# Mixture-of-experts kernel: the expert pipeline runs one expert ahead instead of two, scale factors are spread on VectorE in three pieces, token transposes go by DMA, and the second expert's weights are split inside the routing

## The chip, the core and the metric

The kernel runs on one core of a Trainium2 chip. The metric is the device time of one execution in microseconds (us): 732.28 us is the median of three runs of the kernel before (731.65 to 732.44). Of the core's engines the text says PE for TensorE's matmuls (PEld its weight loads), DVE for VectorE, ACT for ScalarE, POOL for GpSimd and SP for SyncE, whose queue issues the plain DMAs.

## What is computed

Three stages follow each other (sizes: 4 batches, 8 heads, 768 steps, head size 48, so 3072 tokens of 384 numbers; 8 experts of 384 tokens each):

```
# 1 linear attention with decay w and bonus u, per batch and head
y[t] = r[t] @ (state + (u*k[t]) v[t]^T);  state = w*state + k[t] v[t]^T
# 2 greedy routing: all (token, expert) logits in falling order; a token goes to its
#   first expert that still holds fewer than 384 tokens; then per expert
h = max(x[mask] @ w1[e], 0);  x2[mask] = h @ w2[e]
# 3 a shared network with three input matrices (given as 64-bit floats)
out = max(x2 @ v1, x2 @ v2, x2 @ v3) @ w_out
```

## The kernel before

**Halves.** Every product of stages 2 and 3 is made of three fp16 products: a matrix is scaled by a power of two and split into a high half (ACT, `scale=s`) and a low half (DVE, raw times s minus the high half). `product` (L802) multiplies high by high, low by high and high by low. The scale of a matrix needs the largest of its sums of squares over all 128 partitions. `Scales.spread` (L388) finds it with PE: `turn` transposes a column of 128 numbers into a row (L395), DVE takes its maximum (L397), `share` multiplies the one number with a row of ones to bring it to all partitions (L401), and `powering` (L413) makes the power of two with five or six tiny DVE operations.

**Weights.** `weight(e, which)` (L571) prepares one of the two matrices of an expert, as a list of pieces: four looks (ACT squares, L569), the scale, then five or seven splits (high halves L612 on ACT, low halves L615 on DVE). `double(i)` (L626) does the same for one of the shared matrices, with integer operations on DVE that turn 64-bit floats into 32-bit ones (L657 to L672). A `Feed` (L459) holds such pieces in one order; the code around it runs pieces by a budget (`take`), and `ahead` issues the loads of their 768 KB blocks on SP into four slots.

**Order of the work.** In the attention (24 steps, one batch and chunk each) a feed spreads, over steps 1 to 22, both matrices of expert 0, two shared matrices and both matrices of expert 1. Then `Routing.run` (L1284) makes three rounds (`round`, L1078), a chain of small DVE, PE and ACT operations, then `settle` (L1157), which ends with the token lists `ids` (L1221) and a flag; `gather(0)` fetches expert 0's tokens by indirect DMA on POOL, and every engine goes through a branch on the flag (`tc.If`, L1297), whose body is skipped. `idle` puts steps of `inputs` (the scale of the tokens) between the operations of a round. `plan` (L738) builds the feed of what is left: the third shared matrix, w_out, and the weights of experts 2 to 7.

`Experts.run` (L907) then computes. `first(e)` is x @ w1 (72 matmuls of 128x128 by 384), `second(e)` is h @ w2 (72), `third(e)` the three shared matrices (162), `fourth(e)` w_out (54). `turn(e)` (L774) transposes an expert's gathered tokens: nine PE transposes of f32 blocks (L786), then halves on ACT and DVE out of PSUM (L798, L799). Expert 0 and 1 are done to `second` ahead of the loop; in iteration e of the loop (L965) `third(e)` is interleaved with `first(e+2)`, then come `second(e+2)` and `fourth(e)`. The scale of x2 (L861) uses `spread` as well. `side` runs pieces of the feed by a pace worked out from due times, `flush` all that is left up to a tag.

Of the kernel before, what the change touches and what calls it, by code (L numbers as in the profile page):

```python
# [377 lines left out]
class Scales:  # L378


    def __init__(self, tc, pool, K):
        self.nc, self.pool, self.K, self.n, self.psum = tc.nc, pool, K, 0, None
# [5 lines left out]
    def spread(self, peak, then):  # L388
# [15 lines left out]
        return [turn, share]  # L404

# [53 lines left out]
class Feed:  # L459


    SLOTS, AHEAD = 4, 6
# [5 lines left out]
    def add(self, tag, items, early=2):  # L468
# [8 lines left out]
        self.plan += items  # L477

# [37 lines left out]
    def take(self, tag, budget, slot=None, time=1.0, apart=1.0):  # L516

        self.spare = min(self.spare, 0.0) + budget
        self.now += time
        while self.left(tag) and self.spare > 0.3:  # L520
            pe = self.items[self.at][2]
            if pe and (self.now < self.ready or slot not in (None, pe)):
                return
            self.run()
            self.ready = self.now + apart
# [8 lines left out]
class Experts:  # L534
# [4 lines left out]
    def __init__(self, ctx, tc, K, w1, w2, vs, wo, x_dram, out):  # L539
# [4 lines left out]
        self.fix = ctx.enter_context(tc.tile_pool(name="fixed", bufs=1))  # L544
        self.sc = Scales(tc, ctx.enter_context(tc.tile_pool(name="scales", bufs=1)), K)
# [16 lines left out]
    def peak(self, x):  # L562
        p = self.sc.tile()
        self.nc.vector.tensor_reduce(p, x, AX.X, OP.max)
        return p

# [4 lines left out]
    def weight(self, e, which):  # L571

        nc = self.nc
        st = {}
# [16 lines left out]
        def peak():  # L591
            st["peak"] = self.peak(st["peaks"])

        def scale(top):
            st["s"], st["f"] = self.sc.power(top, 3, square=True)
# [12 lines left out]
        def split(n):  # L608
            def go():
                if n < len(parts):  # L610
                    raw, (hi, _) = part(*parts[n])
                    nc.scalar.activation(hi, raw, AF.Copy, scale=st["s"])  # L612
                if n:
                    raw, (hi, lo) = part(*parts[n - 1])
                    nc.vector.scalar_tensor_tensor(lo, raw, st["s"], hi, op0=OP.mult, op1=OP.subtract)  # L615
# [5 lines left out]
        turn, share = self.sc.spread(lambda: st["peak"], scale)  # L621
        return ([(look(j), False, [blocks[j // 2]], 0.9) for j in range(4)] + [(peak, False, blocks, 0.2)]
                + [(turn, 4, blocks, 0.2), (share, 2, blocks, 0.8)]
                + [(split(n), False, uses(n), 0.6 + 0.3 * which) for n in range(len(parts) + 1)])

    def double(self, i):  # L626
# [6 lines left out]
        st, bits = {}, {}  # L633
# [7 lines left out]
        def magnitude(j):  # L641
            a = bits[j] = self.wp.tile([128, 768], I32, name="da", bufs=2)
            nc.scalar.activation(a.bitcast(F32), pair(j)[1].bitcast(F32), AF.Abs, scale=65536.0)
# [5 lines left out]
        def shift(j):  # L649
            def go():  # L650
                total(j - 1)
                if j == 0:
                    magnitude(0)
# [3 lines left out]
                nc.vector.tensor_scalar(x, x, 2.0, None, op0=OP.max)  # L657
# [3 lines left out]
        def low(j):  # L661
            def go():
                if j + 1 < nb:
# [12 lines left out]
        def last():  # L676
            total(nb - 1)

        def peak():
            st["peak"] = self.peak(st["peaks"])  # L680

        def scale(top):
            st["s"], f = self.sc.power(top, 2, square=True, field=self.vf[:, i:i + 1] if i < 3 else None)
            if i == 3:
                self.wof = f
# [13 lines left out]
        turn, share = self.sc.spread(lambda: st["peak"], scale)  # L699
        near = [[blocks[j]] + blocks[j + 1:j + 2] for j in range(nb)]  # L700
        return ([(f(j), False, b, 1.1) for j in range(nb)
                 for f, b in ((shift, blocks[j:j + 1]), (low, near[j]), (sign, blocks[j:j + 1]))]
                + [(last, False, [], 0.1), (peak, False, [], 0.2), (turn, 4, [], 0.2), (share, 2, [], 0.8)]
                + [(split(j), False, [], 0.9) for j in range(nb + 1)])

# [679 lines left out]
```

## Time and profile before

| | |
|---|---|
| median of three runs | 732.28 us |
| the profiled execution: time, span | 732.94 us, 731.2 us |
| attention, up to the logits (L352) | 193 us of the span |
| routing, up to the token lists (L1221) | 193 to 225 us |
| first expert matmul to the last PE work | 231.8 to about 724 us |
| PE, DVE, ACT, POOL busy | 93%, 56%, 44%, 33% of the span |
| mean granted TensorE clock | 0.947 of 2.4 GHz |

The profile is one execution taken by the hardware profiler. Times count from the span's start. The chain that ended last is followed back from the last instruction, at each step to what released it or to the instruction before it on its engine.

### The profile page before, as it was taken

How to read it: one execution, taken by the hardware profiler on the slowest of the kernel's cores; microseconds unless marked ns; L12 is line 12 of the kernel's file. 1: busy time of each engine (PE TensorE's matmuls, PEld its weight loads, DVE VectorE, ACT ScalarE, POOL GpSimd, SP SyncE). 2: the span in 40 equal slices, each digit the busy share in tenths (PEclk: the TensorE clock that was granted, in tenths of full speed). 3: DMA queues.
4: the chain of work that ended last, by engine and by line, in shares of the span. 5: the costliest groups of instructions: out<-in, count | busy, mean ns of one | idle time of the engine just before them, and what ended most of it. 6: DMA issues, size and time to landing. Idle time of an engine off the chain costs nothing.

```text
span 731.2 us, 14572 instructions
## 1 busy us (share of the span) xinstructions
PE 680.0 (93%) x5891; PEld 456.6 (62%) x5891; DVE 411.7 (56%) x954; ACT 322.1 (44%) x657; POOL 238.6 (33%) x264
## 2 busy tenths in 40 slices
PE   5898888999748999999999999999999999999996
PEld 4687667788636755555665666666566665666663
DVE  6779989788673767865453453453535344332120
ACT  3454343454313576655553554544555343232221
POOL 5889777787004200210220220221121021121222
PEclk8999998799756999999999999999999999999999
DMA  5976745562404222421230230321202000000000
GB/s 157 308 230 194 241 138 181 187 199 72 151 1 134 90 85 86 162 87 44 77 119 12 109 118 1 112 83 44 91 30 87 0 33 1 1 34 1 33 1 32
DMA packets 37962, 68.86 MB, mean 94 GB/s; under 512 B 4608, under 2 KB 25216, under 8 KB 37888
## 3 DMA queue, kind: packets, MB, share of 16 engines
q1 hardware_dynamic: 34816, 58.42, 25.0%
q0 software_dynamic: 3072, 9.44, 3.8%
q8 instruction: 48, 0.79, 0.4%
q14 instruction: 26, 0.21, 0.1%
HBM read 58.41 MB, written 9.44 MB: 93 GB/s over the span
## 4 chain that ended last, share of the span: by engine, by line
PE 61%; DVE 3%; issue 2%; ACT 1%; DMA 1%; POOL 1%; POOLq 0%; ACTq 0%; DVEq 0%
PE pg L807 28%; PE ps L807 22%; PE px L893 8%; PE px L401 1%; DVE w L615 1%; PE px L786 1%; DMA stage<-in_moe_w_out_dram 1%; ACT w L612 0%; DVE xt L799 0%; DVE top L877 0%; PE px L395 0%; POOL out_dram L898 0%; DVE x2s L857 0%; POOL gt L880 0%; DVE ht L835 0%
## 5 line engine op out<-in xcount | busy, mean ns | idle before, releaser
L807 PE MATMUL pg<-x2s,v 128*128 128x384 f16 x1296 | 216.8, 326 | 0.0
L807 PEld LDWEIGHTS <-v 128*128 128x128 f16 x1296 | 126.5, 98 | 83.2
L807 PEld LDWEIGHTS <-w 128*128 128x128 f16 x1242 | 115.7, 98 | 70.9 <-issue 1.9
L880 POOL TENSOR_TENSOR gt<-top,gt 128x384 f16<-128x384 f32 x48 | 45.6, 951 | 342.4 <-ACT gt L879 301.5
L877 DVE SCALAR_TENSOR_TENSOR top<-pg,sc,top 128x384 f32<-128x384 f32 x96 | 59.3, 618 | 125.4 <-PE pg L807 122.9
L807 PE MATMUL ps<-ht,w 128*128 128x384 f16 x576 | 95.6, 326 | 0.0
L807 PE MATMUL ps<-xt,w 128*128 128x384 f16 (+1 forms) x540 | 88.5, 317 | 0.8 <-DVE ht L835 0.6
L879 ACT ACTIVATE gt<-top 128x384 f16<-128x384 f32 x48 | 25.1, 523 | 139.3 <-DVE top L877 139.3
L615 DVE SCALAR_TENSOR_TENSOR w<-stage,sc,w 128x512 f16<-128x512 f32 (+1 forms) x80 | 74.2, 950 | 7.4 <-ACT w L612 7.3
L893 PE MATMUL px<-wo,gt 128*128 128x384 f16 x432 | 72.6, 326 | 0.0
L612 ACT ACTIVATE w<-stage,sc 128x512 f16<-128x512 f32 (+1 forms) x80 | 60.8, 797 | 9.6 <-DVE sc L430 9.2
L893 PEld LDWEIGHTS <-gt 128*128 128x128 f16 x432 | 41.8, 98 | 27.0
L569 ACT ACTIVATE junk<-stage 128x768 bf16<-128x768 f32 x64 | 53.4, 835 | 2.8 <-DMA stage<-in_moe_w_dram 2.2
L835 DVE SCALAR_TENSOR_TENSOR ht<-ps,ht 128x384 f16<-128x384 f32 x56 | 30.6, 554 | 32.6 <-ACT ht L834 32.6
L263 ACT ACTIVATE junk<-x 128x384 bf16<-128x384 f32 x24 | 12.6, 523 | 69.5 <-DVE x L262 67.7
L847 DVE TENSOR_REDUCE part<-ps 128x1 f32<-128x384 f32 x24 | 13.4, 556 | 51.4 <-ACT x L846 51.4
L226 PE MATMUL pA<-rt,kt 64*128 64x128 f32 x384 | 34.3, 314 | 7.8 <-DVE am L229 7.5
L898 POOL DMA_INDIRECT out_dram<-o,ids x24 | 23.4, 974 | 44.6 <-ACT o L896 44.6
L226 PEld LDWEIGHTS pA<-rt,kt 64*128 64x128 f32 x384 | 28.4, 212 | 14.3 <-DVE am L229 9.8
L229 DVE TENSOR_TENSOR am<-pA,mask 128x512 f32<-128x512 f32 x48 | 30.7, 680 | 8.9 <-PE pA L226 8.9
L875 ACT ACTIVATE top<-pg,sc 128x384 f32<-128x384 f32 x48 | 27.8, 579 | 16.6 <-PE pg L807 16.2
L202 POOL TENSOR_TENSOR bv<-v,bon 128x384 f32<-128x384 f32 x24 | 23.1, 964 | 31.0 <-DVE bon L200 28.5
(229 smaller groups left out, 916.8 us busy)
## 6 DMA issues: line engine op xcount, KB each, us to landing
stage<-in_moe_w_dram SPq DMA_DIRECT2D x41, 768.0 KB, 4.9
kn<-in_k_dram SPq DMA_DIRECT2D x24, 192.0 KB, 4.6
rn<-in_r_dram SPq DMA_DIRECT2D x24, 192.0 KB, 4.1
v<-in_v_dram SPq DMA_DIRECT2D x24, 192.0 KB, 3.1
rt<-in_rt_dram SPq DMA_DIRECT2D x48, 96.0 KB, 3.2
x_rows<-x SPq DMA_DIRECT2D x24, 192.0 KB, 2.6
stage<-in_moe_w_out_dram SPq DMA_DIRECT2D x3, 768.0 KB, 4.1
xg<-x_rows,ids POOLq DMA_INDIRECT x24, 4.6
```

The lines of the kernel that those rows point to most:

```text
L226: nc.tensor.matmul(pa[s][:, j, :], kt[FULL[s], j * C:(j + 1) * C], rt[FULL[s], j * C:(j + 1) * C], start=True, stop=True, skip_group_check ...
L229: nc.vector.tensor_mul(am[:, s], pa[s], self.mask[:, None, :].to_broadcast([128, NP, C]))
L569: self.nc.scalar.activation(self.K.junk, x, AF.Square, accum_out=total)
L612: nc.scalar.activation(hi, raw, AF.Copy, scale=st["s"])
L615: nc.vector.scalar_tensor_tensor(lo, raw, st["s"], hi, op0=OP.mult, op1=OP.subtract)
L807: nc.tensor.matmul(p[:, rows], w[:, wi, k, cols], x[:, xi, k, rows], start=k == 0 and wi + xi == 0, stop=k == kb - 1 and xi == 1, skip_gro ...
L835: nc.vector.scalar_tensor_tensor(h[:, 1, f], p, 0.0, h[:, 0, f], op0=OP.max, op1=OP.subtract)
L875: nc.scalar.activation(t, p, AF.Copy, scale=self.ratio[i])
L877: nc.vector.scalar_tensor_tensor(t, p, self.ratio[i], top, op0=OP.mult, op1=OP.max)
L879: nc.scalar.activation(gt[:, 0, g], top, AF.Copy)
L880: nc.gpsimd.tensor_sub(gt[:, 1, g], top, gt[:, 0, g])
L893: nc.tensor.matmul(p, gt[:, gi, g, a * 128:(a + 1) * 128], self.WO[:, wi, g, :], start=g == 0 and gi + wi == 0, stop=g == self.KG - 1 and ...
```

## The change

1. `weight(1, 0)` and `weight(1, 1)` leave the attention's feed. Their pieces (41) become `second_matrices`, run by `aside(pieces)`: 4, 2+7 and 3+11 pieces inside rounds 1, 2 and 3, and 11 between `gather(0)` and the branch; the last three go to the feed. There the scale still goes by PE (`fine`), but in eight small pieces; seven of the ten low halves go to POOL in two operations each. The steps of `inputs` that are left run after `gather(0)` too.
2. In the planned feed (`early` is False) scales go by `around`: a column maximum, four 32x32 DVE transposes, a row maximum (`collect`), one DVE transpose of the broadcast number and two copies (`share`), the power of two (`end`). The x2 scale does the same, and its halves become three more pieces, spread by `step()`.
3. `turn(e)` for e of 1 and more makes the halves first, in token order, and then three `dma_start_transpose` on SP (128 x 768 fp16 each).
4. The loop runs one expert ahead: `third(0)` alone, `first(e+1)` beside `third(e)` for e from 1 to 6. w_out is due 1.5, ahead of expert 2.
5. In `double`, the maximum with 2.0 moves from DVE to POOL for matrices of the planned feed.

```diff
+    def around(self, peak, powers, kind):
+        ... (a, c, d), b = self.blocks[kind], self.wide
+        def collect():
+            peak(a[:, :1])
+            for q in range(4):
+                nc.vector.transpose(b[:32, 32 * q:32 * q + 32], a[32 * q:32 * q + 32])
+            nc.vector.tensor_reduce(c[:32, :1], b[:32], AX.X, OP.max)
+        def share():
+            nc.vector.transpose(d[:32], c[:32, :1].to_broadcast([32, 32]))
+            nc.vector.tensor_copy(d[32:64, :1], d[:32, :1])
+            nc.vector.tensor_copy(d[64:, :1], d[:64, :1])
+        def end():
+            for _ in powers(d[:, :1]):
+                pass
+    def fine(self, peak, powers):
+        ...
+        return [start, turn, share] + [lambda: next(st["g"])] * 4 + [last]
...
+            if calm:
+                nc.gpsimd.tensor_scalar(t, raw, st["s"], None, op0=OP.mult)
+                nc.gpsimd.tensor_sub(lo, t, hi)
...
+    def second_matrices(self):
+        (look, scale, _, upper, lower), (look2, scale2, split2, _, _) = (self.weight(1, n, True) for n in range(2))
+        return (look + scale[:5] + look2 + scale[5:] + scale2[:2] + [upper(0), upper(1), lower(0, True), upper(2), lower(1, True),
+                upper(3), lower(2, True), upper(4), upper(5)] + [lower(n) for n in range(3, 6)] + scale2[2:] + [split2(n, True) for n in range(5)])
...
+        if not blocks:
+            for a in range(3):
+                t = self.act.tile([128, 2, DM], F16, name="xr", bufs=3)
+                nc.scalar.activation(t[:, 0], self.XG[e % 2][a], AF.Copy, scale=K.xs)
+                nc.vector.scalar_tensor_tensor(t[:, 1], self.XG[e % 2][a], K.xs, t[:, 0], op0=OP.mult, op1=OP.subtract)
+                nc.sync.dma_start_transpose(xt.rearrange("p t j n -> p (t j) n")[:, :, a * 128:(a + 1) * 128],
+                                            t.rearrange("p t n -> p (t n)"))
...
         for e in range(E):
-            n = e + 2
+            n = e + 1
-            first = self.first(n) if n < E else iter(())
+            first = self.first(n) if e and n < E else iter(())
...
-        self.idle(1 if src is self.K.raw else 3)
+        self.idle(1 if n == 0 else 0)
+        self.aside((4, 7, 11)[n])
...
         then()
         for _ in other:
             pass
+        aside(11)
+        self.aside = lambda pieces: None
         with tc.If(bad != 0) as _:
...
-    for which in range(2):
-        feed.add(0, X.weight(1, which))
```

## Rows read from the trace of the kernel before

**Rows 1.** The chain that ended last, shares of the span by engine and by line (the page's part 4).

```profile
PE 61%; DVE 3%; issue 2%; ACT 1%; DMA 1%; POOL 1%; POOLq 0%; ACTq 0%; DVEq 0%
PE pg L807 28%; PE ps L807 22%; PE px L893 8%; PE px L401 1%; DVE w L615 1%; PE px L786 1%; DMA stage<-in_moe_w_out_dram 1%; ACT w L612 0%; DVE xt L799 0%; DVE top L877 0%; PE px L395 0%; POOL out_dram L898 0%; DVE x2s L857 0%; POOL gt L880 0%; DVE ht L835 0%
```

**Rows 2.** Busy time of each engine in the expert stages: stretch, its length, then PE, PEld, DVE, ACT, POOL busy with instruction counts, granted clock, DMA share, GB/s.

```profile
231.70:721.00 489.30, 485.40 (x3082) 297.50 (x3082) 230.82 (x521) 224.86 (x434) 89.70 (x112) 1.00 0.18 59
```

**Rows 3.** The chain in one expert's turn, in order of time: start, length, what.

```profile
484.89 0.98 PE px L786 x9
...
488.80 4.39 PE pg L807 x27
...
507.92 0.31 PE px L401 x2
...
524.42 0.11 PE px L395
```

**Rows 4.** PE's groups from 246 us to the end: busy us, mean ns of one, idle before.

```profile
L401 PE MATMUL px<-sc,onesf 1*128 1x1 f32 x44 | 8.3, 256 | 0.7 <-DVE xt L799 0.7
L786 PE MATMUL px<-identf,xg 128*128 128x128 f32 x63 | 8.3, 274 | 0.9 <-DVE sc L416 0.9
L395 PE MATMUL px<-identf,sc 128*1 128x128 f32 x22 | 6.0, 272 | 0.1
```

**Rows 5.** The stretch after the first experts' matrices begin to interleave, columns as in rows 2.

```profile
276.00:309.00 33.00, 30.79 (x193) 18.96 (x192) 25.87 (x58) 22.09 (x40) 4.97 (x5) 1.00 0.41 138
```

**Rows 6.** The same stretch, the chain in order of time: the longest piece.

```profile
284.43 5.21 DMA stage<-in_moe_w_out_dram
```

**Rows 7.** The attention's steps 1 to 23, columns as in rows 2.

```profile
27.00:190.80 163.80, 149.00 (x2522) 125.12 (x2521) 138.18 (x245) 78.40 (x167) 124.79 (x107) 0.93 0.56 179
```

**Rows 8.** The nine of these steps in which DVE is busy for 95% or more, the sum over them.

```profile
sum 79.50, PE 70.48 PEld 59.58 DVE 78.43 ACT 35.31 POOL 59.43; mean PE 7.83 PEld 6.62 DVE 8.71 ACT 3.92 POOL 6.60
```

**Rows 9.** DVE's groups of the feed in the attention, 60 to 185 us, shapes apart: busy us, mean ns.

```profile
L615 DVE SCALAR_TENSOR_TENSOR w<-stage,sc,w 128x512 f16<-128x512 f32 x6 | 7.2, 1217 | 0.0
L615 DVE SCALAR_TENSOR_TENSOR w<-stage,sc,w 128x768 f16<-128x768 f32 x4 | 5.6, 1418 | 0.0
L397 DVE TENSOR_REDUCE sc<-pX 1x1 f32<-1x128 f32 x5 | 1.4, 275 | 1.0 <-PE pX L395 1.0
L423 DVE TENSOR_SCALAR sc<-sc 128x1 int32<-128x1 int32 x5 | 0.8, 154 | 0.2
```

**Rows 10.** The same operation in the expert stages, 400 to 600 us, where POOL is mostly idle.

```profile
L615 DVE SCALAR_TENSOR_TENSOR w<-stage,sc,w 128x512 f16<-128x512 f32 x21 | 15.6, 764 | 0.8 <-ACT w L612 0.7
```

**Rows 11.** POOL's groups in the attention, 60 to 185 us.

```profile
L126 POOL TENSOR_TENSOR rt<-rt,tr 128x512 f32<-128x512 f32 x16 | 24.3, 1521 | 0.0
L192 POOL TENSOR_TENSOR rk<-rk,ub 128x384 f32<-128x384 f32 x16 | 20.1, 1257 | 1.3
L183 POOL TENSOR_TENSOR kp<-kn,tkn 128x384 f32<-128x384 f32 x15 | 18.4, 1228 | 2.1 <-PE pK L281 2.1
L191 POOL TENSOR_TENSOR rk<-rn,kn 128x384 f32<-128x384 f32 x16 | 18.2, 1139 | 0.0
L202 POOL TENSOR_TENSOR bv<-v,bon 128x384 f32<-128x384 f32 x18 | 17.6, 978 | 26.1 <-DVE bon L200 23.5 <-DVE sc L564 2.6
```

**Rows 12.** The routing in order of time, merged instructions: start, length, engine, line, operation, [idle before].

```profile
200.49 0.58 PE L732 MATMUL px<-sc,onesf 1*128 1x1 f32 x2
...
207.32 0.58 PE L1147 MATMUL pt<-vals,onesf 96*128 96x16 f32 x2 [2.32 <-DVE sc L425]
207.94 0.17 DVE L1151 TENSOR_SCALAR cut<-pt 128x8 f32<-128x8 f32 x1 [0.45 <-PE pt L1147]
...
217.82 0.46 ACT L1175 ACTIVATE ahead<-later,heldc 96x200 f16<-96x200 f16 x1 [4.62 <-DVE heldc L1173]
...
221.05 1.19 POOL L1203 TENSOR_TENSOR rhs<-col,token 128x576 f16<-128x576 f16 x1 [36.03 <-ACT gap L1209]
...
224.86 0.18 DVE L1221 TENSOR_SCALAR ids<-pn 128x24 int32<-128x24 f32 x1 [0.29 <-PE pn L1219]
```

**Rows 13.** The branch behind the routing, on PE's queue: durations in ns (min, median, max), first and last start.

```profile
L1297 PEldq COMPARE_BRANCH  x1: 3563/3563/3563, 226.0 to 226.0; - x1
```

**Rows 14.** The chain at the second and third block of expert 0's tokens, in order of time.

```profile
234.90 0.46 issue
...
235.74 1.05 issue
```

**Rows 15.** DMA issues (the page's part 6): KB each, median us from issue to landing.

```profile
v<-in_v_dram SPq DMA_DIRECT2D x24, 192.0 KB, 3.1
kn<-in_k_dram SPq DMA_DIRECT2D x24, 192.0 KB, 4.6
stage<-in_moe_w_dram SPq DMA_DIRECT2D x41, 768.0 KB, 4.9
```

**Rows 16.** One `second` of expert 0 on PE (timeline): its 72 matmuls.

```profile
247.51 11.86 PE L807 MATMUL ps<-ht,w 128*128 128x384 f16 x72
```

**Rows 17.** What follows `third` (page, part 5): the evacuations of its PSUM banks on ACT and DVE, and the low half on POOL.

```profile
L875 ACT ACTIVATE top<-pg,sc 128x384 f32<-128x384 f32 x48 | 27.8, 579 | 16.6 <-PE pg L807 16.2
L877 DVE SCALAR_TENSOR_TENSOR top<-pg,sc,top 128x384 f32<-128x384 f32 x96 | 59.3, 618 | 125.4 <-PE pg L807 122.9 <-ACT top L875 1.0 <-PE px L395 0.8
L880 POOL TENSOR_TENSOR gt<-top,gt 128x384 f16<-128x384 f32 x48 | 45.6, 951 | 342.4 <-ACT gt L879 301.5 <-issue 40.9
```

More of the change, by code (lines that the diff above doesn't have):

```diff
@@ L459 @@
 class Feed:
[L462 removed]
+    SLOTS, AHEAD, LAG = 4, 6, 1.4
     def __init__(self):
@@ L560, in block, with scaled, peak, then @@
         return b
[L562 to L565, printed above, removed]
     def square(self, x, total):
         self.nc.scalar.activation(self.K.junk, x, AF.Square, accum_out=total)
-    def weight(self, e, which):
+    def scaled(self, st, column, powers, blocks):
+        if self.early:
+            def peak():
+                st["m"] = self.sc.tile()
+                column(st["m"])
+            def then(top):
+                for _ in powers(top):
+                    pass
+            turn, share = self.sc.spread(lambda: st["m"], then)
+            return [(peak, False, blocks, 0.2), (turn, 4, blocks, 0.2), (share, 2, blocks, 0.8)]
+        collect, share, end = self.sc.around(column, powers, "weights")
+        def done():
+            end()
+            self.mark(st)
+        return [(collect, st, blocks, 1.2), (share, False, blocks, 0.6), (done, False, blocks, 0.8)]
+    def mark(self, st):
+        st["sent"] = self.feed.now
+    def weight(self, e, which, parted=False):
         nc = self.nc
-        st = {}
+        st = {"sent": 0.0}
         if which == 0:
@@ L588, in go, with column, powers @@
                 self.square(blocks[j // 2].get()[:, j % 2 * 768:j % 2 * 768 + 768], st["peaks"][:, j:j + 1])
-            return go
[L591 to L595, printed above, removed]
+                if j == 3 and not self.early:
+                    self.mark(st)
+            return go
+        def column(out):
+            nc.vector.tensor_reduce(out, st["peaks"], AX.X, OP.max)
+        def powers(top):
+            yield from self.sc.powering(top, 3, True, st)
             st["w"] = self.wpool[e % 2].tile([128, 2, kb, n], F16, name=f"w{which}", bufs=1)
@@ L619, in uses @@
             return [blocks[parts[i][0]] for i in (n - 1, n) if 0 <= i < len(parts)]
[L621 to L624, printed above, removed]
+        looks = [(look(j), False, [blocks[j // 2]], 0.9) for j in range(4)]
+        if parted:
+            return (looks, [(x, False, blocks, 0.2) for x in self.sc.fine(column, powers)],
+                    lambda n, calm: (split(n, calm), st if n == 0 and not self.early else False, uses(n), 0.9),
+                    lambda n: (lambda: upper(n), False, uses(n), 0.7), lambda n, calm=False: (lambda: lower(n, calm), False, uses(n + 1), 0.8))
+        return (looks + self.scaled(st, column, powers, blocks)
+                + [(split(n), st if n == 0 and not self.early else False, uses(n), 0.6 + 0.3 * which)
+                   for n in range(len(parts) + 1)])
     def double(self, i):
@@ L677, in last, with column, powers @@
             total(nb - 1)
[L679 to L683, printed above, removed]
+            if not early:
+                self.mark(st)
+        def column(out):
+            nc.vector.tensor_reduce(out, st["peaks"], AX.X, OP.max)
+        def powers(top):
+            if i < 3:
+                st["f"] = self.vf[:, i:i + 1]
+            yield from self.sc.powering(top, 2, True, st)
             if i == 3:
-                self.wof = f
+                self.wof = st["f"]
         def halves(j):
@@ L697, in split @@
             return go
-        turn, share = self.sc.spread(lambda: st["peak"], scale)
         near = [[blocks[j]] + blocks[j + 1:j + 2] for j in range(nb)]
[L701 to L704, printed above, removed]
+        return ([(lambda: magnitude(0), False, blocks[:1], 0.3)] * (not early)
+                + [(f(j), False, b, 1.1) for j in range(nb)
+                   for f, b in ((shift, blocks[j:j + 1] if early else near[j]), (low, near[j]), (sign, blocks[j:j + 1]))]
+                + [(last, False, [], 0.1)] + self.scaled(st, column, powers, [])
+                + [(split(j), st if j == 0 and not early else False, [], 0.9) for j in range(nb + 1)])
     def room(self, i):
@@ L1326, in body @@
         feed.add(0, X.double(i))
-    for which in range(2):
-        feed.add(0, X.weight(1, which))
     feed.close()
@@ L1337, in body @@
     with ExitStack() as rctx:
-        routing.run(rctx, X.inputs(), X.sc, lambda: X.gather(0))
+        routing.run(rctx, X.inputs(), X.aside, X.sc, lambda: X.gather(0))
     X.open(ctx)
```

204 lines of the change are left out of this document (131 added, 73 removed).

## The prediction

> **What bounds the kernel now.** I read the chain that ended last first. PE is 61% of it, nearly all of that in lines 807 and 893, the expert products [rows 1]. Then the busy time of each engine in the expert stages: PE is busy for 485.4 of 489.3 us at full clock, DVE for 230.8 and ACT for 224.9, so DVE and ACT are under half used [rows 2]. The reader should see that two thirds of the kernel are a queue of PE work with almost no holes: there only two things give time back, PE instructions that vanish and the few holes. Next the attention. Over its steps 1 to 23 DVE is busy for 138.2 of 163.8 us, POOL for 124.8 [rows 7]; in nine steps, 79.5 us together, DVE is busy for 78.4 [rows 8]. So about half of the attention (79.5 / 163.8 = 0.49) is bound by DVE, the rest by POOL, PE and waits. Last the routing: a chain of small operations in which ACT and POOL idle for long stretches (4.6 us ahead of line 1175, 36 us ahead of line 1203) [rows 12], closed by a branch.
>
> The sum is made against the profiled execution's own time, 732.94 us (span 731.2 and 1.7 around it). The median of the runs is 0.66 us lower; I take the difference from it.
>
> **Token transposes leave PE.** Experts 1 to 7 have nine PE transposes each, 63 in all [rows 4]; nine take 0.98 us of the chain [rows 3]. 7 x 0.98 = **-6.9 us**. The halves stay: one ACT and one DVE operation per token block as before. The three DMA transposes per expert wait on SP behind the halves. For experts 2 to 7 they are issued inside `third(e)` for a `first` one iteration later, some 58 us of PE work (489.3 / 8 is 61); that hides any landing time seen here. Only expert 1 is tight: its cover is `second(0)`, 11.9 us [rows 16]. No row shows a DMA transpose. The nearest are plain transfers of the same 192 KB, which land in 3.1 to 4.6 us [rows 15]. In a pipeline the three land some 7 us after `first(0)` ends, with about 2 us for the halves: hidden. One after another it is 3 x 4.6 + 2 = 15.8, 3.9 us too late. I take 0 and keep 0 to 3.9.
>
> **Scales leave PE.** From the start of the expert stages there are 22 column transposes and 44 passes of the one-number matmul [rows 4]; one scale takes 0.11 + 0.31 us of the chain [rows 3]. 22 x 0.42 = **-9.2 us**. What DVE gets for it is about seven more operations per scale at some 0.15 us (the tiny-operation row of rows 9), 22 x 7 x 0.15 = 23 us more on an engine that has 258 us free in that stage [rows 2]: 0. No DVE transpose is in the trace; between the 0.15 of a tiny operation and the 0.28 of a 128-number maximum [rows 9] it changes nothing.
>
> **One expert ahead.** It moves PE work without changing its amount. Its effect is on due times: ahead of `third(0)` the feed now owes one shared matrix, before it was one shared matrix and w1 of expert 2. In the stretch where this crowded, PE is busy for 30.8 of 33.0 us [rows 5], and the chain there runs through ACT and DVE and a 5.2 us wait for a block of w_out [rows 6]. At most 2.2 us are to be had; since w_out now comes in `third(0)` and can block ACT in the same way, I take **-1.0** (0 to -2.2). The evacuation of `third`, 0.58 us on ACT and two of 0.62 on DVE [rows 17], fits the 4.39 us that PE needs for one group [rows 3], also where nothing is interleaved.
>
> **The attention without expert 1's weights.** DVE loses six low halves of 1.22 us, four of 1.42, and two scales of about 1.2 us (0.15 + 0.28 + five tiny ones) [rows 9]: 7.3 + 5.7 + 2.4 = 15.4 us. ACT loses eight looks and ten high halves, but is busy for 78 of 164 us [rows 7], so that counts for nothing. POOL's own work stays: a step has 1.52 + 1.26 + 1.23 + 1.14 + 0.98 = 6.1 us on POOL [rows 11], against 7.1 us for a mean step, so a step cannot shrink far. If DVE bound everything the gain would be 15.4; if POOL and PE took over at once it would be 0. The feed spreads what is left over the same steps, so I count the share of the time that DVE bounds: 15.4 x 0.49 = **-7.5** (0 to -15.4).
>
> **The routing with expert 1's weights.** Three costs, none of them in the trace as such.
> (a) In round 2, `share` and two power steps now stand ahead of `cut`. DVE must wait there for the one-number matmul, which PE runs behind the `pt` matmul; in round 1 of before such a pair follows by 0.5 us [rows 12]. With the two operations of 0.15 us `cut` comes at about 208.85 instead of 207.94: +0.9.
> (b) ACT's high halves and POOL's low halves fill idle time. Six high halves fit the 4.6 us ahead of line 1175 by a hair [rows 12]; POOL's three low halves should be done as line 1203 needs it. DVE's operations beside a busy POOL are longer: 1.22 against 0.76 us for the same 128x512 low half [rows 9, 10]. A dozen operations of settle by up to 0.25 us is 3 us; nothing slower is 0. I take +0.8, since most of settle's operations are far smaller than a low half.
> (c) Eleven pieces and the five last steps of the tokens' scale stand between `ids` and the branch, and that is no wait: each engine takes the branch only after them. DVE: five tiny ones 0.8, three low halves 2.3 [rows 10], the maximum 0.3; then PE's one-number matmul 0.6. PE's branch, at 226.0 before, starts at about 229.9, and it lasts 3.56 us [rows 13]. So the first transposes come 3.9 us later. About 2 us of that are given back, since PE afterwards waited 0.46 and 1.05 us for later token blocks, with a transpose between [rows 14], which will then lie there. ACT has two high halves of the second matrix to issue ahead of its own branch and may be later still. I take +2.3 (0 to 4).
> Sum **+4.0** (+1 to +7).
>
> **Sum.** -6.9 - 9.2 - 1.0 - 7.5 + 4.0 = -20.6. 732.94 gives 712.3 for a profiled execution, 732.28 gives **711.7 us**. All ends together: 732.3 - 6.9 - 9.2 - 2.2 - 15.4 + 1 = 699.6, and 732.3 - 6.9 - 9.2 + 7 + 3.9 = 727.1.
>
> **Rivals.**
> A. *The attention does not shrink* (0.13). For it: POOL's 6.1 us of a 7.1 us step, and the light steps that run with DVE far from full. Against: half of the time with DVE at 98%. Time 732.3 - 20.6 + 7.5 = 719.2.
> B. *DVE's whole time comes back and the routing hides the rest* (0.10). For it: the heavy steps dropped the granted clock (0.93 over the stretch [rows 7]), which evener steps would mend. Time 732.3 - 6.9 - 9.2 - 1.0 - 15.4 + 1 = 701.
> C. *The transposes of expert 1 land behind `second(0)`* (0.10). For it: no row bounds a transpose from above. Against: the plain transfers of rows 15. Time 715.6 by the rows' worst, about 725 at three times their time.
> The Trainium skill, VectorE: DVE Perf Modes, section The three transpose paths, gives 1309 ns for one 128x128 transpose by DMA against 390 on TensorE; an estimate from that page for 18 blocks in a row is 23.6 us, and expert 1 would be 13.7 us late, 725 in all; no row here shows it.
> D. *SP becomes the bound* (0.05), the one that ends slower. SP issues in order; if a transpose holds it, the blocks of the feed queue behind, ACT stands at a look or a magnitude whose block is not there, and PSUM isn't emptied. The one such wait in the trace is 5.2 us [rows 6]. PE has about three groups of PSUM, some 4.4 us, in hand, so it decides when a turn holds SP for some 8 us or more longer than a block's 4.9 us takes to land [rows 15]; with 5.2 us lost in each of six turns it is 31 us, 711.7 + 31 = 743.
> That part of the change doesn't do what it says is in (c): the last pieces lie behind the routing's waits, not in them. E. *POOL's low halves hold up settle* (0.05). For it: the longer low halves beside a busy POOL [rows 9, 10]. Against: POOL's three should end as settle begins. If six of settle's operations each wait for one POOL operation of 0.95 us [rows 17], (b) is 5.7 instead of 0.8, and the time 716.6.
> The Trainium skill, SBUF — State Buffer, section Who interferes with whom, speaks for E: a DVE operation with two SBUF inputs and a POOL operation that reads SBUF exclude each other for a whole instruction; the longer low halves agree with that, while by rows 9 and 10 alone the price is the 0.25 us each that (b) counts at most.
> That part of the change doesn't do what it says is in (c): the last pieces lie behind the routing's waits, not in them. The remaining 0.57 is the forecast, some 704 to 718.
>
> **How the numbers follow.** A measurement of this kernel tells about 0.2% (1.5 us) from no change. The range 702 to 722 takes in the forecast, A, E and the near part of C; it leaves out half of B, the far end of C and D, about 0.15. Faster needs over 1.5 us: all but D and a sliver, 0.93; within 0.2% 0.02; slower 0.05.
>
> **What would show it.** No L786 transposes for experts 1 to 7 and no one-number matmuls in the expert stages; that stretch, 489.3 us, near 472 plus any holes. The attention's end, at 193.0, near 185.5. `ids` some 1.7 us later after that end than the 31.8 us of before, and the first expert product 8 to 11 us after `ids` (6.7 before). PE without a hole at the start of `first(1)`. Wrong would be: an attention that ends at 192 (A) or 178 (B), a hole there (C), ACT waiting for stage blocks in each expert (D).

## The result

The changed kernel takes 740.81 us (median of 4 runs, 740.4 to 742.66), the kernel before 732.36 beside it (4 runs, 731.65 to 734.35): ratio 1.0116, 95% interval 1.009 to 1.0142 (as for all ratios here). It is slower by 8.5 us; 711.7 was forecast. The profiled execution took 740.82 us, its span 739.1.

**Four cuts through the span.** The line that copies the attention's last result, the one that makes `ids`, and the first expert product are in both traces. After the change, in order of time (start, length, engine, line, operation, what the engine had waited for):

```profile
181.28 0.33 ACT L352 ACTIVATE raw<-lg 128x192 f32<-128x192 f32 x1 [0.93 <-PE lg L306]
...
196.68 0.16 DVE L470 TENSOR_SCALAR sc<-py 128x1 int32<-128x1 int32 x1 [1.08 <-PE py L451]
...
196.94 0.16 DVE L1292 TENSOR_SCALAR cut<-pt 128x8 f32<-128x8 f32 x1
...
202.95 1.16 POOL L707 TENSOR_TENSOR w<-da,w 128x512 f16<-128x512 f32 x1 [2.16 <-ACT w L700]
...
203.10 1.03 DVE L1281 SCALAR_TENSOR_TENSOR pick<-pick,least 96x1 f32<-96x1 f32 x1
204.09 1.56 POOL L706 TENSOR_SCALAR da<-stage,sc 128x512 f32<-128x512 f32 x1
204.16 0.65 DVE L1284 TENSOR_TENSOR vals<-same,pick 96x16 f32<-96x16 f32 x1
...
205.96 1.14 DVE L1295 TENSOR_TENSOR pen<-nl,cut 128x192 f32<-128x192 f32 x1
...
207.14 0.73 DVE L1296 SCALAR_TENSOR_TENSOR nl<-pen,nl 128x192 f32<-128x192 f32 x1
...
216.59 0.18 DVE L1362 TENSOR_SCALAR ids<-pn 128x24 int32<-128x24 f32 x1 [0.30 <-PE pn L1360]
...
227.82 1.51 PE L925 MATMUL px<-identf,xg 128*128 128x128 f32 x6 [6.59 <-ACTq L1440]
...
229.49 1.13 PE L943 MATMUL ps<-xt,w 128*128 128x128 f16 x9 [0.16 <-ACT xt L934]
```

| part of the span | before, us | after, us | difference | forecast |
|---|---|---|---|---|
| start to the attention's end (L352) | 193.0 | 181.3 | -11.7 | -7.5 |
| to `ids` [rows 12] | 31.9 | 35.3 | +3.4 | +1.7 |
| to the first expert product | 6.9 | 12.9 | +6.0 | +2.3 |
| to the end of the span | 499.4 | 509.6 | +10.2 | -17.1 |

The forecast of the third row has some 2 us in it that PE was to get back just behind the first product. All ahead of the experts together gained 2.3 us, as against 3.5 forecast; the miss lies in the last row, 27.3 us.

**Where in the expert stage.** PE's products of the output matrix come once per expert. After the change three in a row start 58.50 us apart:

```profile
395.50 8.94 PE L1034 MATMUL px<-wo,gt 128*128 128x384 f16 x54
454.00 8.94 PE L1034 MATMUL px<-wo,gt 128*128 128x384 f16 x54
512.50 8.94 PE L1034 MATMUL px<-wo,gt 128*128 128x384 f16 x54
```

Before, they start 61.05 apart:

```profile
402.26 3.09 PE L893 MATMUL px<-wo,gt 128*128 128x384 f16 x18
...
463.31 3.09 PE L893 MATMUL px<-wo,gt 128*128 128x384 f16 x18
```

The 2.55 us per expert are a little more than the two PE terms promised (16.1 / 7 = 2.3). The loss is earlier. Windows of the changed kernel, columns as in [rows 2]:

```profile
229.50:255.50 26.00, 26.00 (x239) 19.38 (x239) 8.72 (x16) 7.48 (x16) 10.48 (x8) 0.93 0.39 100
255.50:288.00 32.50, 16.92 (x80) 8.60 (x79) 20.41 (x41) 15.32 (x28) 18.02 (x9) 0.73 0.31 106
288.00:300.20 12.20, 12.20 (x67) 6.91 (x67) 7.15 (x22) 2.65 (x7) 0.48 (x1) 0.88 0.11 41
300.20:324.00 23.80, 19.60 (x117) 11.12 (x116) 18.26 (x55) 14.11 (x25) 5.95 (x6) 1.00 0.36 63
324.00:345.90 21.90, 18.39 (x100) 10.16 (x100) 13.91 (x43) 12.37 (x24) 4.94 (x8) 0.92 0.41 136
232.00:345.00 113.00, 89.71 (x572) 53.14 (x570) 67.33 (x173) 51.48 (x97) 37.98 (x29) 0.89 0.33 91
345.90:660.00 314.10, 314.08 (x1933) 188.76 (x1931) 167.30 (x442) 156.07 (x305) 61.18 (x76) 1.00 0.26 74
```

and one of the kernel before:

```profile
232.00:345.00 113.00, 109.17 (x759) 69.47 (x757) 76.40 (x166) 67.30 (x130) 16.50 (x17) 0.99 0.29 91
```

From 346 us on PE has no hole at all. Between 232 and 345 it idles 23.3 us against 3.8, and runs at a granted clock of 0.89 against 0.99, so that busy time times clock is 79.8 against 108.1: 28.3 us of full-speed work less, which covers the 27.3 us. The reader should also see the row above the hole: in 229.5 to 255.5 PE is full while DVE works 8.7 us and ACT 7.5. The feed stands still, and then the work comes all at once. The longest waits of PE between 232 and 345 are for DVE, whose evacuations of PE's banks (`ht`) stand behind pieces of the feed:

```profile
PE ps L943 <- DVE ht L971: 10.1, 2, 9.9
PE pg L943 <- DVE ht L971: 4.7, 1, 4.7
```

### The profile page after: what moved, and what is told of

Same layout as the page of the kernel before. It is cut to its first block, busy times and chain, and to the rows that moved or that the text cites. A ratio compares the mean times of both kernels' runs of the same rounds, so it can differ in the third digit from the quotient of the medians.

```text
span 739.1 us, 14533 instructions
## 1 busy us (share of the span) xinstructions
PE 664.2 (90%) x5762; PEld 441.1 (60%) x5762; DVE 434.4 (59%) x1097; ACT 321.8 (44%) x657; POOL 275.3 (37%) x284
## 4 chain that ended last, share of the span: by engine, by line
PE 57%; DVE 4%; issue 3%; ACT 2%; POOL 2%; POOLq 0%; DVEq 0%; ACTq 0%
PE pg L943 26%; PE ps L943 23%; PE px L1034 8%; DVE top L1018 1%; ACT junk L633 1%; POOL da L751 1%; ACT w L700 0%; DVE da L780 0%; DVE wo L815 0%; DVE v L815 0%; POOL gt L1021 0%; POOL w L707 0%; POOL da L706 0%; DVE ht L971 0%; POOL out_dram L1039 0%
## 5 line engine op out<-in xcount | busy, mean ns | idle before, releaser
L943 PEld LDWEIGHTS <-w 128*128 128x128 f16 x1242 | 119.1, 100 | 91.9 <-issue 22.2
L943 PE MATMUL ps<-ht,w 128*128 128x384 f16 x576 | 97.8, 332 | 10.8 <-DVE ht L971 9.9
L709 DVE SCALAR_TENSOR_TENSOR w<-stage,sc,w 128x512 f16<-128x512 f32 (+1 forms) x73 | 66.3, 933 | 6.1 <-ACT w L700 6.1
L982 ACT ACTIVATE x<-ps 128x384 f32<-128x384 f32 x24 | 11.8, 490 | 52.7 <-PE ps L943 52.7
L226 PE MATMUL pA<-rt,kt 64*128 64x128 f32 x384 | 32.1, 303 | 1.7 <-DVE am L229 1.5
L126 POOL TENSOR_TENSOR rt<-rt,tr 128x512 f32<-128x512 f32 x22 | 32.7, 1485 | 1.7 <-DMA rt<-in_rt_dram 1.7
```

Source lines behind the costliest of these rows:

```text
L126: (engine or self.nc.gpsimd).tensor_mul(self.RT[i], self.RT[i], self.tr)
L226: nc.tensor.matmul(pa[s][:, j, :], kt[FULL[s], j * C:(j + 1) * C], rt[FULL[s], j * C:(j + 1) * C], start=True, stop=True, skip_group_check ...
L943: nc.tensor.matmul(p[:, rows], w[:, wi, k, cols], x[:, xi, k, rows], start=k == 0 and wi + xi == 0, stop=k == kb - 1 and xi == 1, skip_gro ...
```

## The experiments

A code reading gave the first theory. The pieces that the routing runs aside are taken out of order by the feed's `run`, which charges their cost to `spare`; `take` starts each side from the negative `spare`. Adding up the kernel's own costs, the account stands at -21.2 when the expert stages begin, and the sides run nothing until it is paid back. The ratios below are each with the kernel before on the same chip; its median there was 732.5 to 734.7 us.

**e1: the debt.** At the end of `aside`:
```
+        self.feed.spare = 0.0
```


> The changed kernel with one line more: after the pieces that run inside the routing the feed's budget is set back to 0. Theory 1 (debt: the 38 pieces run in the routing are charged to the budget, which stands at -21.2 as the expert stages begin, so no piece runs for some 26 us and then two shared matrices are crammed into the next 60): ACT and DVE work from the first expert on, PE's idle time of 23 us between 255 and 346 us falls to under 6, time 710 to 718 against 740.8. Theory 2 (the operations moved to POOL, some 2.2 us each, stand in the path of ACT and DVE): the holes stay with little less, time over 730.

**e2: GpSimd's part.** In the planned feed, GpSimd's maximum (L751) and the low halves of expert 1's second matrix back on DVE; the debt stays:
```
-                nc.gpsimd.tensor_scalar(a, a, 2.0, None, op0=OP.max)
+                nc.vector.tensor_scalar(x, x, 2.0, None, op0=OP.max)
-    [split2(n, True) for n in range(5)]
+    [split2(n, False) for n in range(5)]
```


> The changed kernel with the planned feed's POOL operations back on DVE: the maximum with 2.0 of the shared matrices, and the low halves of the second matrix of expert 1; the debt stays. Theory 1: the feed still idles for 26 us and is crammed after, only the chains get shorter, 732 to 739. Theory 2: the holes go, under 722.

**e3: both edits.**


> Both edits, budget set back to 0 and POOL's operations of the planned feed back on DVE. Theory 1: as e1 within 4 us, 708 to 717. Theory 2: as e2, and e1 well above both.

**e4: e1, and no pieces ahead of the branch.**
```
-        self.aside((4, 7, 11)[n])
+        self.aside((4, 7, 9)[n])
-        aside(11)
```
(and the start of the second matrix's scale goes with its splits into the planned feed.)


> The edit of e1, and the 11 pieces ahead of the branch (with the start of the second matrix's scale) left to the feed of the expert stages; only the steps of the tokens' scale stay ahead of the branch. If those pieces delay the branch, the stretch from the token lists to the first expert product falls from 12.8 us to 8 or less, and the time is up to 5 us under e1 unless the crowded feed gives it back. If the branch is slow for another reason (instruction fetch beside the block loads), the stretch stays over 11 us.

| | us, median | ratio (interval) | first product | from there to the span's end | PE idle in 232 to 345 |
|---|---|---|---|---|---|
| before | 732.36 | | 231.8 | 499.4 | 3.8 |
| after | 740.81 | 1.0116 (1.009 to 1.0142) | 229.5 | 509.6 | 23.3 |
| e1 | 728.58 | 0.993 (0.9895 to 0.9964) | 231.6 | 499.9 | 14.7 |
| e2 | 736.04 | 1.0023 (0.999 to 1.0055) | 228.5 | 506.0 | 20.3 |
| e3 | 725.41 | 0.986 (0.981 to 0.9911) | 231.6 | 492.3 | 11.0 |
| e4 | 737.5 | 1.0043 (1.0006 to 1.0081) | 224.7 | 512.3 | 26.1 |

The stages here and below are read from one execution each, and that can lie off the median: e1's took 733.2 us, 4.6 more than its median, e6's 3.5 less, and those of p1b, p2 and p3 3.1 to 4.0 less. The debt costs 12.2 us in the median, 9.7 in the expert stage. GpSimd's operations cost 3.6 in that stage with the debt (509.6 to 506.0) and 7.6 without (499.9 to 492.3); in the medians it is 4.8 and 3.2. Together the two are 17.3 of the 27.3, 15.4 in the medians; how they share it is known to some 4 us only. The expectations of e1, 710 to 718, and of e3, 708 to 717, fell; e2's, 732 to 739, held: the debt is the largest single cause, not the whole. e4 settles the routing's third term. Before the branch stand no pieces, and from `ids` (217.66) to the first product (224.65) there are 7.0 us again, 6 less than after. But the eleven pieces, put into the planned feed, cost more than that: the kernel is 8.9 us slower than e1. One window of e4:

```profile
255.00:270.00 15.00, 4.66 (x18) 2.25 (x18) 7.34 (x10) 5.22 (x9) 11.43 (x6) 0.66 0.42 139
```

PE works 4.7 of 15 us, with GpSimd the busiest engine.

**e5: the order.** e3, and the third shared matrix wholly ahead of w_out's first pieces:
```
-        parts = [(1, self.double(i), 0) for i in late]
+        parts = [(1, self.double(i), None) for i in late]
```


> The changed kernel without the debt, with the VectorE forms of e3 (725.4), and with all pieces of the third shared matrix ahead of the pieces of expert 1's second matrix, so that not two matrices fall before the second expert's last products. Theory: what is left of the loss is the order and the crowding of these pieces on VectorE: 716 to 721, the holes of 255 to 330 us down from some 14 to some 6 us. Rival: the holes are the price of having one expert's weights less ahead, wherever the pieces stand: 724 to 727, the holes only move.

**e6: e5 with e4's edit.**


> e5 and, as in e4, no pieces between ids and the branch (the start of the second matrix's scale goes into the planned feed with its splits). By the routing term: about 6 us from ids to the first product come back, so 6 us below e5 if the planned feed has room for the 11 pieces (then TensorE stays at over 90% in 255 to 300 us); with no room they cost there what they gain, within 2 us of e5; in e4, with the feed still crowded, they cost 9 us net.

e5: 721.46 us, ratio 0.9831 (0.9784 to 0.9877), expert stage 490.5, idle 8.7. e6: 729.74, 0.9935 (0.9904 to 0.9967), idle 17.3. e5's expectation names expert 1's second matrix; what its edit moves behind the third shared matrix is w_out's first pieces. So the order was worth another 4 us in the medians (1.8 in the expert stage), just short of the 716 to 721 expected. Even with GpSimd out of the way the planned feed has no room for the eleven pieces: the 5.1 us won from `ids` to the first product (12.4 in e5, 7.3 in e6) are more than lost again in holes, and e6 is 8.3 us slower, where at most 2 were expected.

**e7: the lock.** In the changed kernel's rows above, DVE's `pick` takes 1.03 us in round three, beside GpSimd's low halves; in rounds one and two it takes 0.21. e7 is e5 with these three low halves on DVE:
```
-    lower(0, True), ... lower(1, True), ... lower(2, True)
+    lower(0), ... lower(1), ... lower(2)
```


> e5 with the three low halves that stand on GpSimd inside the routing (two GpSimd instructions each) put on VectorE, one instruction each. Theory of the lock: the routing's two-input VectorE instructions of round three (pick 1.03 us, vals 0.65, pen 1.14, nl 0.73 in the changed kernel) fall to their 0.21, 0.17, 0.36, 0.36 of the rounds before; three extra VectorE instructions of 0.6 to 1.0 us stand in the waits instead, so the time from logits to ids falls by 1 to 2.5 us and the whole by as much, 719 to 721. Rival: the instructions are as long without GpSimd beside them (ScalarE or the transfers slow them): then the durations stay and the time rises by 1 to 3 us.

Round three of e7:

```profile
201.38 0.22 DVE L1279 SCALAR_TENSOR_TENSOR pick<-pick,least 96x1 f32<-96x1 f32 x1
201.64 0.17 DVE L1282 TENSOR_TENSOR vals<-same,pick 96x16 f32<-96x16 f32 x1
...
204.17 0.36 DVE L1293 TENSOR_TENSOR pen<-nl,cut 128x192 f32<-128x192 f32 x1
204.56 0.36 DVE L1294 SCALAR_TENSOR_TENSOR nl<-pen,nl 128x192 f32<-128x192 f32 x1
```

The four fall from 3.55 us together (1.03, 0.65, 1.14, 0.73) to 1.11. Logits to `ids` is 33.8 us against 35.4 in e5. The kernel takes 719.84 us, within the 719 to 721 expected, 0.9817 (0.9748 to 0.9885): the fastest that leaves no work out, faster than both kernels, though its gain over e5 is within the intervals. By the Trainium skill, SBUF — State Buffer, section Who interferes with whom, a DVE operation with two SBUF inputs contends with a GpSimd operation that reads SBUF. These rows agree: the four are 0.4 to 0.8 us longer beside GpSimd operations of 1.2 to 1.7 us. `pick` and `pen` end 0.0 and 0.2 us after a GpSimd operation does; `vals` and `nl` end 0.8 and 0.7 us before the one beside them does.

**e8: is it DVE's sum?** e7 with one DVE instruction per block left out of the planned feed's last shared matrix and w_out:
```
+                if early:
                     nc.vector.scalar_tensor_tensor(bits[j], pair(j)[0], 29, bits[j], ...)
```


> e7 with one VectorE instruction per block left out in the planned feed's last shared matrix and w_out (the one that joins the low 29 bits of the words; 6 instructions of 0.955 us, 5.7 us of VectorE in 229 to 346; so the output is not the reference's in the low bits). Theory: from 240 to 300 us VectorE sets the pace there (14.6, 14.2 of 15 us busy in two stretches of e7), so most of the 5.7 us comes back, 714 to 717 against 719.8, and the idle time of TensorE in 240 to 345 (8.7 us in e7) falls to some 4. Rival: the holes are set by the order in which pieces are given out and by ScalarE ahead of VectorE, not by VectorE's sum: 719 to 721, holes unchanged.

718.58 us, 0.979 (0.9708 to 0.9872), which can't be told from e7; 714 to 717 was expected. In 232 to 345 PE is busy 104.33 us, in e7 104.30. The theory fell: the 8.7 us of holes that stay are not DVE's total. In e7, PE's waits in 240 to 345 us are these:

```profile
PE pg L941 <- ACT top L1014: 5.0, 3, 2.6
PE ps L941 <- DVE ht L969: 3.3, 1, 3.3
```

They are evacuations of PE's own banks that stand in ACT's and DVE's queues behind pieces; which order would free them was not found.

**p1, p1b: the transposes alone**, put into the kernel before (two experts ahead, its own feed): for `not blocks`, ACT and DVE write the halves `xr` and
```
+                nc.sync.dma_start_transpose(xt...[:, :, a * 128:(a + 1) * 128], t...)
```
with two blocks of `xr` in p1, three in p1b. For room p1b, and all of p1c, p1d, p3 and p3d with it, has two output blocks instead of three; behind the first output product p1b's PE has no hole from it.


> The kernel before with the DMA transposes of the token halves alone (two blocks of halves instead of the change's three, for room). The prediction's own term: 7 x 0.98 us off TensorE in a stage that TensorE bounds, 6.9 us, so 725.4 against 732.3. The rival that has the transposes late at the start of the next expert: 732 to 741, with TensorE waiting at the first matmuls of each expert. If the sum's PE terms are right and the loss lies in the feed alone, 724 to 727.

> The kernel before with the DMA transposes alone, now with three blocks of token halves as in the change (the room is taken from the output blocks: two instead of three). Theory: the 28 us that p1 lost came from its two blocks only (ScalarE's write of the third halves waited 4.7 us for the first DMA transpose, and the ht copies stood behind it), so the prediction's term holds: 723 to 728, with no wait of ScalarE for xt<-xr and the experts' period down from 61.05 to about 60.1 us. Rival: the DMA transposes themselves come too late for the next expert's first products: 735 to 755, with TensorE waiting on them.

p1: 760.54 us, 1.0365 (1.0316 to 1.0413), slower than any expectation. Its chain in one expert's turn, in order of time:

```profile
383.97 1.23 PE pg L817 x8
385.19 4.34 DMA xt<-xr
...
389.64 0.62 ACT xr L785
...
390.29 0.62 DVE xr L786
390.91 0.48 DVE ht L845
...
391.43 0.62 PE ps L817 x2
```

ACT's third `xr` waits until the first block's transpose has been read out; `ht` stands behind it on DVE, PE behind that, in each expert. With three blocks (p1b) the wait is gone and an expert's turn, from one first output product to the next, is 60.07 us, 0.98 less than before, exactly the term. But p1b takes 736.35 us, 1.0049 (1.0015 to 1.0083): slower than before.

**p2: the scales alone** in the kernel before, all but the first ones made on DVE:
```
-        turn, share = self.sc.spread(lambda: st["peak"], scale)
+        turn, share = ... if self.early else self.sc.around(lambda: st["peaks"], scale, "weights")
```


> The kernel before with the planned scales (the weights' and the layer's) on VectorE alone, without TensorE; in two pieces where the change has three; two experts ahead as before. The prediction's own term: 22 x 0.42 us off TensorE, 9.2 us, so 723. If the extra small VectorE instructions delay the feed so that TensorE waits for pieces, 728 to 733; with TensorE never waiting for the feed in the trace, 722 to 725.

**p3: p1b and p2 together**, so the change's two PE savings without its order.


> The kernel before with both parts that take work off TensorE (scales on VectorE, DMA transposes with three blocks), the weights still split two experts ahead, and nothing else of the change. Theory: what was lost in the change is the one-ahead order with its feed; without it the two PE terms come in full, 6.9 and 9.2 us off 732.3: 714 to 719. Rival: the small VectorE instructions of the scales and the token halves crowd VectorE in any order, and holes of some 8 us stay between 240 and 350 us: 722 to 727.

p2: 732.11 us, 0.9995 (0.9956 to 1.0034); p3: 733.15, 0.9996 (0.9951 to 1.004). p1b and p3 miss their theories, and p2 misses its 722 to 725 but lands in the 728 to 733 put down for a feed that is delayed. Split at the start of the first output products (341.21 us in before, 344.52, 344.25 and 348.85 in p1b, p2 and p3; the last expert's start at 715.58, 714.96, 711.69, 712.36):

| | first expert product to first output product | from there to the last expert's output | PE idle in 232 to 345 |
|---|---|---|---|
| before | 109.4 | 374.4 | 3.8 |
| p1b | 114.7 (+5.2) | 370.4 (-3.9) | 9.3 |
| p2 | 114.1 (+4.6) | 367.4 (-6.9) | 9.3 |
| p3 | 118.0 (+8.6) | 363.5 (-10.9) | 14.8 |

The second column adds up (3.9 + 6.9 = 10.8). Four experts' transposes are 4 x 0.98 = 3.9, as forecast; the 14 scales that lie there cost PE 0.49 each, where the forecast had 0.42. The first column gives back 4.6 to 8.6 us, with no debt, no GpSimd and no expert order in play, and the medians of p2 and p3 show no gain at all.

In p2, without any DMA transpose, PE's longest waits in that stretch are for evacuations that stand behind other work on DVE, the feed's pieces among it:

```profile
PE ps L834 <- DVE ht L862: 7.2, 2, 5.0
```

**p1c, e9: who issues.** p1b and e7 with the transposes on ACT's queue:
```
-                nc.sync.dma_start_transpose(
+                nc.scalar.dma_start_transpose(
```


> p1b with the DMA transposes issued from ScalarE's queue instead of SP's, so that SP issues weight blocks alone. In p1b the first block of 252.85 us was issued behind three transposes (before: 248.68) and landed 6.36 us later; TensorE then waited 5.0 us for the scale. Theory of SP's order: the blocks go out at 248 to 249 us again, the 5.0 us shrink below 2, and the idle time of TensorE in 232 to 345 falls from 9.3 us towards before's 3.8; the time falls to 725 to 730, less what ScalarE loses by waiting at the transposes (at most some 3 us per expert, hidden in the later experts). Rival: it is the transposes' traffic that slows the blocks, on any queue: landing stays over 6 us, idle time stays at 9, 730 to 736.

> e7 with the DMA transposes issued from ScalarE's queue. By the same theory SP's blocks of 249 and 302 us go out some 5 us earlier, and TensorE's idle time in 240 to 345 (8.7 us) falls by 2 to 5: 715 to 718 against 719.8. By the rival, that ScalarE's queue ahead of the products sets these holes (TensorE waits 5.0 us for top from ScalarE), it gets worse: 721 to 726.

775.15 us, 1.0586 (1.0523 to 1.0649), and 765.31, 1.0438 (1.0405 to 1.0471): slower than any expectation. The chain of p1c:

```profile
252.47 0.52 ACT xr L785
...
253.66 1.34 ACTq L787
...
256.35 1.24 ACTq L787
...
258.93 1.23 ACTq L787
```

A transposing DMA holds its queue 1.2 to 1.3 us, and it waits there for DVE's half: from the first write to the end of the third transpose ACT's queue is taken for 7.7 us (252.47 to 260.16), ahead of PE's evacuations. SP does send its blocks earlier (in p1c four weight blocks have gone out by 267.0 us, in p1b the fourth at 281.17), but with ACT held neither run shows what that is worth.

**p1d, p3d: off SP at one place.** Expert 1's tokens stay on PE:
```
-        if not blocks:
+        if e > 1:
```


> p1b with expert 1's tokens on TensorE as before and the DMA transposes for experts 2 to 7 only (6 x 0.98 us off TensorE, 5.9). Theory of SP's order: the weight block that stood behind the first three transposes goes out at some 248.7 us again instead of 252.85, the 5.0 us wait of TensorE for the scale goes, and the idle time of TensorE in 232 to 345 falls from 9.3 us to 4 to 6: 726 to 729 (span 726 to 727 against 730.6 of p1b). Rival: the feed in this stretch has no slack whatever the block does, TensorE waits for what it has saved: idle time stays at 8 to 9, 730 to 734.

> p3 with expert 1's tokens on TensorE as before. Theory of SP's order: the 7.2 us wait of the chain for the block of 253.66 us goes, the idle time in 232 to 345 falls from 14.8 to some 10: 722 to 726 (span 723 to 725 against 728.0 of p3). Rival, no slack in the feed: span 727 to 729.

In the kernel before, SP's queue sends four weight blocks between 221.24 and 258.38; in p1b it sends transposes between them, the first three at 248.74, and stands at the transposes for their halves:

```profile
221.24 37.14 SPq L556 DMA_DIRECT2D stage<-in_moe_w_dram  x4
```

```profile
248.74 4.06 SPq L787 DMA_TRANSPOSE xt<-xr  x3
252.85 2.19 SPq L556 DMA_DIRECT2D stage<-in_moe_w_dram  x3
276.98 4.13 SPq L787 DMA_TRANSPOSE xt<-xr  x3
281.17 0.57 SPq L556 DMA_DIRECT2D stage<-in_moe_w_dram  x1
```

SP's waits at the transposes in p1b, 231 to 345 us (total, times, longest):

```profile
SPq L787 <- DVE xr L786: 53.0, 3, 21.9
```

So the block of 252.85 is the one that left at 221.24 before, and that of 281.17 the one that had left by 258.4. The expectations of p1c and p1d tie the 5.0 us wait for the scale to the first; p1b's chain has it behind the second:

```profile
281.17 5.07 DMA stage<-in_moe_w_dram
...
288.41 0.37 PE px L395
```

p1d and p3d set only the first free. In p1d it goes out at 222.57, and PE has no hole from 240 to 285 us. But:

```profile
255.00:270.00 15.00, 15.00 (x94) 8.93 (x92) 10.10 (x22) 9.88 (x21) 0.00 (x0) 1.00 0.20 57
270.00:285.00 15.00, 15.00 (x94) 8.95 (x92) 11.99 (x35) 11.71 (x24) 0.00 (x0) 1.00 0.28 44
285.00:300.00 15.00, 10.07 (x52) 5.46 (x51) 6.61 (x18) 6.75 (x11) 0.91 (x1) 0.89 0.42 155
```

p1b's windows were 13.04, 13.43 and 11.59 in these three stretches. The large hole has not gone: it is 4.9 us (285.62 to 290.55) where p1b had 5.0 (283.43 to 288.41), and the second block still goes out behind transposes, at 283.26. The idle time of 232 to 345 is 8.2 instead of 9.3. p1d: 736.29 us, 1.0029 (0.9989 to 1.0069). p3d: 729.94, 0.9941 (0.9913 to 0.997), idle 12.3 instead of 14.8, span 728.2. The theory's times (726 to 729 and 722 to 726) fell; p1d's idle time and p3d's span are the rival's. So the first block is worth 1 to 2.5 us of idle time, and the second, on which p1b's largest hole rests by its chain, was not set free in any run but those that held ACT instead.

## Why the prediction was wrong

**The step that failed** is the feed in the expert stages, which the sum holds only as "One expert ahead", put at -1.0 (0 to -2.2) with the reason that it moves PE work without changing its amount. It was read as due times alone. What changed is the feed itself: the pieces run aside put its account at -21.2 (9.7 us of expert stage in e1, 12.2 in the medians), GpSimd was given pieces there (7.6 us, e3 against e1; 3.2 in the medians), and w_out's first pieces came ahead of the third matrix's last (e5 against e3: 1.8 us of expert stage, 4 us of median). The first two come from other parts of the change, 1 and 5, and the sum has no term for either: the routing's costs end at the first product. The three take the expert stage from 509.6 to 490.5, against 482.3 forecast. No bound in the sum covered a loss here; D, the only rival that was slower, put it on SP. The order alone did not lose: p3, with two experts ahead and the same two PE savings, has 497.2, 6.7 more than e5, though the two differ in how fine the pieces are as well.

**The PE terms** (-6.9 and -9.2) were right as amounts, the scales even somewhat low, and wrong as time. Behind the first output product each expert is shorter by what they said. But [rows 2] was read as one queue of PE work, and its first 110 us are not: there PE was full at [rows 5]'s 30.8 of 33 us only because the feed just kept up, and the chain of that stretch ran through ACT, DVE and a block [rows 6]. p1b, p2 and p3 show that a us off PE there becomes a wait, and more than that: in p1b for a block behind transposes, in p2 for DVE. Of 16.1 us, p3's profiled execution keeps 2.2 (its expert stage is 497.2 us, 728.0 less 230.8, against 499.4), its median none. The 8.7 us of holes left in e5 and e7 are waits for ACT and DVE; no run removed them.

**Attention**: -11.7 against -7.5 (0 to -15.4). The direction and the range held. The other kernels with the changed attention end it at 179.5 to 184.5 us, those with the old one at 191.5 to 195.9: each end scatters by 4 to 5 us, but the two groups lie 7 us apart; rival A is out. Why it gained more than DVE's share of the time was not tried. B's reason does not stand in the trace of before: of the nine heavy steps six have a granted clock of 1.00, and the three with 0.85 to 0.92 are those in which PE has idle time.

**Routing**: (a) as said: DVE waits 1.08 us for the one-number matmul, and `cut` comes 1.39 us after its matmul's start where it came after 0.62. (b) was +0.8 and is about +2.4: E had the mechanism, GpSimd holding up DVE, but it struck round three's four operations and not settle's. (c) was +2.3 and is +6.0 (e4: 7.0 us from `ids` to the first product without the pieces, as before). The branch was to start 3.9 us later; it starts 4.3 us after `ids` instead of 1.1, so 3.2 later, where 3.9 was worked out. But it was to last 3.56 as in [rows 13], and on PE's queue it was 2.6 us longer (durations in ns, start):

```profile
L1440 PEldq COMPARE_BRANCH  x1: 6173/6173/6173, 220.9 to 220.9; - x1
```

**C**, late transposes of expert 1, is out: SP issues three from 245.55 on, and the first product that reads all three blocks starts at 255.26, right behind `second(0)`; only p3 shows 1.4 us of it. From the 1309 ns that the Trainium skill, VectorE: DVE Perf Modes, section The three transpose paths, gives for one block, 18 blocks would take an estimated 23.6 us; the trace shows at most 9.7 for them, so the measurement decides against it here. **D** saw a true mechanism and priced it wrongly. SP stands far longer than the 8 us that D asked for, in the changed kernel's first two turns 17.6 and 29.7 us, since a transpose waits in the queue for its halves (205 to 325 us):

```profile
SPq L917 <- DVE xr L916: 47.3, 2, 29.7
```

But the changed kernel's chain from 255 to 320 us has no wait for a block that stood there, and from 346 us on PE has no hole. Where such a block does cost time is in p1b and p1d, 5.0 and 4.9 us at one place.

## What to carry to other kernels

A busy share near 100% says that an engine is full, not that it is the only bound: ask of each stretch what would happen if this engine were faster, and look at the feed that must be done by the same point. Work put into another stage's waits is charged to someone's account; follow the account (budgets, due times, queue order) into the stage that comes after. A saving in a part with a deadline should be counted only behind that deadline. Before something that waits for its input goes into a queue, look at what stands behind it there.

## What the hardware showed that was not expected

- PE's branch took 3523 to 3857 ns in the kernel before, e4, e6 and p2, where no pieces stood ahead of it, and 5717 to 6437 in all eight kernels with the eleven pieces. In after, e5 and e7 SP, DVE, ACT and PE take the branch within 1.2 to 2.2 us of each other; in the kernel before, e6 and p2 they are spread over 5.4 to 6.1. That the one causes the other was not tried.
- A DMA transpose of 128 x 768 f16 holds the issuing queue 1.22 to 2.18 us (median 1.25 of the changed kernel's 21) and lands 2.7 to 6.1 us after its issue. Before that it holds the queue for as long as its input is missing, in the changed kernel up to 29.7 us.
- GpSimd's `tensor_scalar` on 128 x 768 f32 takes 2.20 us where DVE's low half, which does its work and the subtraction, takes 1.02.
